# First token group of an attention + feed-forward kernel in units of two f-tiles for 256 tokens, then f-tiles of 512 tokens, six of them in three fp32r passes

## Chip, cores and metric

One core of one Trainium2 chip. The metric is the device time in microseconds of one execution of the program; the median of three executions is given. A profiled execution has a span (first to last instruction) and a time of its own.

## What is computed

The reference runs a recurrent attention (per head a 48 x 48 state that decays by `w`, takes in k v, and is read by r; `u` weighs the token's own k v), and then a feed-forward layer over its output:

```
for t in range(768):                       # 4 sequences, 8 heads of 48
    cur = u*k[t] (x) v[t];  y[t] = r[t] . (state + cur);  state = w*state + k[t] (x) v[t]
x = y as 3072 tokens x 384
h = x @ w_in                               # 384 x 2048
g = h * tanh(log1p(exp(h)))
out = g @ w_out                            # 2048 x 384
```

The two matrices arrive as 64-bit floats, everything else as 32-bit ones.

## The kernel before

**Tokens and groups.** The attention goes in 24 steps `s`; a step makes 128 token columns of x (two chunks of 64). Four steps make a group of T = 512 tokens; there are six groups `g`. The feed-forward layer goes by f-tiles of 128 of the 2048 hidden rows, NF = 16 in a group, so tile number n = 16 g + f. For a tile, `up_tile` (L965) makes h in a PSUM buffer of tag `hp` (two buffers), `evacuate` (L984) copies it to `hb` on ACT or DVE, `gate` (L989) runs sigmoid, arctan and sine on ACT over two tiles (1024 columns; L863, L866, L869, two of them with a table load) and a multiply on DVE (L874 in group 0, L876 later), and `down_tile` (L1019) adds the tile's products to the three accumulators `acc0` to `acc2`. `ffn` (L1078) emits up n, then down n - 6 (LAG), in this order.

**Precision.** In group 0 both products are single fp32 matmuls with whole fp32 weights (L852 up, L896 down); the trace shows each as two records. In groups 1 to 5, x, g and the weights are split into a high and a low fp32r part, and a product is three matmuls (`three`, L828, records at L830).

**Weights.** Each matrix comes in eight pieces of two f-tiles (WG = 2). A piece is loaded as 64-bit numbers (`load_weight`, L334), made fp32 by `convert` (L339: one ACT instruction, L351, and three on DVE, L355, L357, L359), and later split for the fp32r passes by `split` (L364: ACT L372, DVE L374). W_ORDER (L327) is the order of the pieces. A split takes the buffer of the piece before it, so it waits until that was used for the last time.

**The start.** Steps 0 and 1 are loaded first, then pieces of the matrix and steps 2 and 3 (FIRST, L69). Until all four steps are there, group 0 can't take whole 512-token tiles. So `early_pieces` (L929) runs f-tiles 0 to 3 in halves of 256 tokens (records at L945): the half of steps 0 and 1 as soon as these are there, the other half after step 3. EARLY puts two of the four in `hp` and two in the accumulators' banks `acc0` and `acc1`. The attention of steps 0 to 3 is: `dots` (L476), `scores` (L527), `spread_y` (L577, the outputs, in the banks `yt` and `acc2`), `finish` (L741: copies and adds on ACT L760 and DVE L763 make x), and `first_state` (L716, products at L711, copied at L729 and L735). A step's outputs wait for `y` of the step before, which frees the banks. Idle stretches of TensorE that the planner sees are filled with products of zeros (`keep_warm`, L259).

**What sets the order.** The instructions of PE, ACT, DVE, Pool and SP stand in an order that a planner, `Flow` (L91), writes out at build time. Every activity is a thread that asks for an engine with an estimated cost (`dve`, `act`, `pe`, L152 to L161, `tile_cost` L926) and has a rank; of the requests that could start earliest the lowest rank goes first. Each engine then takes its instructions strictly in that order. Steps 4 to 7 are spread over group 0's tiles by `place` (L797) between the shares LO0 and HI0.

Of the kernel before, what the change touches and what calls it, by code (L numbers as in the profile page):

```python
# [67 lines left out]
EARLY = ("hp", "hp", "acc0", "acc1")  # L68
# [21 lines left out]

class Flow:  # L91
# [4 lines left out]
    def __init__(self, free):  # L96
        self.free, self.now, self.events = dict(free), 0.0, {}
        self.live, self.parked, self.fill = [], {}, None

# [35 lines left out]
    def run(self):  # L135
        while self.live:
# [5 lines left out]
            t, th, d = min(todo[e], key=lambda t: (t[0], t[1][0]))  # L142
            self.live = [x for x in self.live if x is not th]
            if e == "pe" and self.fill and t - self.free[e] > WARM_MIN:
                self.fill(t - self.free[e] - LAT)
            self.free[e] = t + d
            self.now = th[1] = t + d + (DMA_LAT if e == "sp" else LAT)
# [4 lines left out]
def dve(cols, fast=False):  # L152
    return {"dve": 0.14 + cols / (1900 if fast else 950)}
# [6 lines left out]
def pe(us):  # L160
    return {"pe": us}  # L161
# [3 lines left out]
def rwkv_mish_kernel(ctx, tc, rkT, rkN, vN, wT, w_in, w_out, consts, rkF, vF, wF, uF, outT):  # L165
# [72 lines left out]
    def token_table():  # L238
# [8 lines left out]
        yield pe(1.0)  # L247
# [10 lines left out]

    def keep_warm(n, out=None):  # L259

        for _ in range(n):
# [12 lines left out]
    idle = ps.tile([128, 512], F32, name="idle", tag="hp", bufs=2)  # L274
    keep_warm(WARM0 - 2)

    flow = Flow(FREE)
# [8 lines left out]
    def check_range():  # L286
# [28 lines left out]
        yield pe(0.3)  # L315
# [11 lines left out]
    W_ORDER = sorted(((i, f) for i in range(2) for f in range(NW)), key=lambda w: w[1] * WG + w[0] * W_SHIFT)  # L327
    raws, whole, parts = {}, {}, {}

# [4 lines left out]
    def load_weight(c):  # L334
        raws[c] = raw = wpool.tile([128, WE, 2], U32, name="wraw", tag="w")
        nc.sync.dma_start(raw, weights(c))
        flow.set(f"issued{c}")
# [26 lines left out]
    def split(c):  # L364
        yield f"whole{c}"
        if c:
            yield f"split{c - 1}"
            yield "used%d,%d" % W_ORDER[c - 1]
        e = whole[W_ORDER[c]]
        yield act(WE)  # L370
        parts[W_ORDER[c]] = w = wpool.tile([128, 2, WE], F32R, name="w", tag="w")
# [3 lines left out]
        flow.set(f"split{c}")  # L375
        flow.set("w%d,%d" % W_ORDER[c])
# [85 lines left out]
    def dots(s):  # L462
        if s < N_SQ:
# [10 lines left out]
            yield pe(1.2)  # L474
# [57 lines left out]
    def attend(s):  # L532
        if s <= B:
# [4 lines left out]
            yield pe(0.6)  # L538
# [101 lines left out]
    def outputs(s):  # L640
# [14 lines left out]
        else:  # L655
            if s >= 2:
                yield f"out{s - 2}"
                yield f"spread{s - 2}"
            engine = yield {**act(96), "dve": 0.25}
# [5 lines left out]
        if not rows:  # L665
            yield pe(0.9 if s < 2 else 1.4)
            ys = spread_y(s)
        else:
            yield pe(2.1 - 0.4 * last)
# [4 lines left out]
        if not rows:  # L674
            flow.start(first_state(s), s - 899.5)
# [40 lines left out]
    def first_state(s):  # L716
        if s >= 2:
            yield f"early{len(EARLY) - 1}"
# [3 lines left out]
        yield pe(0.5)  # L722
# [18 lines left out]
    def finish(s, ys):  # L741
# [9 lines left out]
        if not g:  # L751
            xk = x[:, :, b, 0].rearrange("m k (b t) -> m k b t", b=2)
            parts_y = [y[:, : 2 * KT * CK].rearrange("m (k b t) -> m k b t", k=KT, b=2) for y in ys]
            if s < 2:
                for h in range(2):
                    yield act(192)
                    nc.scalar.copy(out=xk[:, :, h], in_=parts_y[h][:, :, h])
            else:
                yield act(384)
                nc.scalar.copy(out=xk, in_=parts_y[1])  # L760
                for k, h in ((slice(0, 2), slice(0, 2)), (2, 0)):
# [55 lines left out]
    def hp_free(cost=None):  # L817
# [5 lines left out]
        while len(hp_log) >= 2 and hp_log[-2] not in flow.events:  # L823
            yield hp_log[-2]
            yield pe(cost)
# [19 lines left out]
    def up(o, j, event=None):  # L845
        f, T = o.f + j, o.T
        hp = hp_tile("hp", event)
        for k in range(KT):
            fs = slice((k * WG + f % WG) * 128, (k * WG + f % WG + 1) * 128)
            if o.x.dtype == F32:  # L850
                e = whole[0, f // WG]
                nc.tensor.matmul(hp[:, :T], lhsT=e[:, fs], rhs=o.x[:, k, :, 0], start=k == 0, stop=k == KT - 1)  # L852
            else:
                w = parts[0, f // WG]
                three(
                    hp[:, :T], w[:, 0, fs], w[:, 1, fs], o.x[:, k, :, 0], o.x[:, k, :, 1], k == 0, k == KT - 1
                )
# [30 lines left out]
    def down(o, j):  # L888
        f = o.f + j
        for mt in range(KT):  # L890
# [4 lines left out]
            if o.x.dtype == F32:  # L895
                nc.tensor.matmul(a, lhsT=whole[1, f // WG][:, ws], rhs=o.gf[:, j], start=f == 0, stop=f == NF - 1)  # L896
            else:
                w = parts[1, f // WG]
                three(a, w[:, 0, ws], w[:, 1, ws], o.gh[:, j], o.gl[:, j], f == 0, f == NF - 1)
# [26 lines left out]
    def tile_cost(g):  # L926
        return pe(9 * (T + 30) / 2400 if g else 3 * 4 * T / 2400)

    def early_pieces(n):  # L929

        yield f"e0,{n // WG}"
        if n == 3:
            yield "TKn"
        hp = None
        for b in range(0, B, 2):
            yield f"x{b}"
            yield f"x{b + 1}"
            yield pe(1.3)
            flow.fill = None
            if hp is None:  # L940
                hp = hp_tile("hp", f"h{n}") if EARLY[n] == "hp" else ps.tile([128, 512], F32, name="hp", tag=EARLY[n])
            at = slice(b * C, (b + 2) * C)
            for k in range(KT):
                fs = slice((k * WG + n % WG) * 128, (k * WG + n % WG + 1) * 128)
                nc.tensor.matmul(  # L945
                    hp[:, at], lhsT=whole[0, n // WG][:, fs], rhs=xs[0][:, k, b : b + 2, 0], start=k == 0, stop=k == KT - 1
                )
        flow.set(f"early{n}")
        emitted(n, hp)
# [336 lines left out]
```

## Time and profile before

| what | value |
|---|---|
| median of three executions | 501.92 us (501.25 to 502.31) |
| the profiled execution: its time / its span | 499.15 us / 497.4 us |
| TensorE busy | 484.1 us (97%), mean granted clock 0.988 |
| ScalarE busy | 407.5 us (82%) |
| VectorE busy | 356.6 us (72%) |

The time of the profiled execution is 1.75 us above its span; it is 2.77 us below the median. PE stands for matmuls, PEld for weight loads, which lie beside them. L numbers are lines of the kernel before.

### The profile page before, as it was taken

Reading aid. Unit: us, or ns where it says so; the run is one execution under the profiler, and the core shown is the slowest. Engines: PE = TensorE matmul, PEld = TensorE weight load, DVE = VectorE, ACT = ScalarE, POOL = GpSimd, SP = SyncE. Lnnn points to the kernel's source line nnn. Section 1 sums busy time; section 2 is a strip of 40 time slices with the busy share of each in tenths; the row PEclk is TensorE's granted clock in tenths of the full one; section 3 lists DMA queues with packets and bytes.
Section 4 is the critical chain, followed back from the end, with each engine's and each line's share of the span. In section 5 each row is a group of like instructions: output and inputs, shape, how many; then the busy total and the mean of one; then the engine's idle time right before and its main releaser. Section 6 shows DMA issues by size and latency. Waiting matters only on the chain.

```text
span 497.4 us, 11220 instructions
## 1 busy us (share of the span) xinstructions
PE 484.1 (97%) x4779; PEld 369.4 (74%) x4782; DVE 356.6 (72%) x567; ACT 407.5 (82%) x524; POOL 5.4 (1%) x28
## 2 busy tenths in 40 slices
PE   8979999999999999999999999999999999999994
PEld 4766455556678888888888888888888888888872
DVE  6869987978689885687775887685787456465432
ACT  3747988868789898787788899988879988899791
POOL 2000000000000000000000000000000000000000
PEclk9789999999999999999999999999999999999999
DMA  8998122330243021343224445223454103130002
GB/s 314 410 410 359 54 96 91 117 110 5 96 128 111 35 84 29 96 139 108 92 86 144 165 139 184 80 89 150 161 167 138 63 15 129 65 127 1 2 0 70
DMA packets 19978, 60.43 MB, mean 122 GB/s; under 512 B 3088, under 2 KB 3984, under 8 KB 19920
## 3 DMA queue, kind: packets, MB, share of 16 engines
q1 hardware_dynamic: 17184, 54.80, 32.0%
q10 hardware_dynamic: 2736, 4.84, 2.6%
q8 instruction: 39, 0.64, 0.5%
q14 instruction: 19, 0.16, 0.1%
HBM read 52.94 MB, written 4.72 MB: 116 GB/s over the span
## 4 chain that ended last, share of the span: by engine, by line
PE 91%; ACT 3%; DMA 3%; DVE 1%; issue 1%; SPq 0%; ACTq 0%; DVEq 0%
PE hp L830 33%; PE acc L830 30%; PE acc L896 8%; PE hp L852 6%; PE pa L527 2%; PE hp L945 2%; DMA rk<-in_rkT_dram 1%; PE yt L602 1%; PE yh L711 1%; DMA rkn<-in_rkN_dram 1%; PE y L577 1%; PE pa L602 1%; PE pa L614 1%; PE yh L614 1%; PE idle L262 1%; PE pa L476 1%
## 5 line engine op out<-in xcount | busy, mean ns | idle before, releaser
L830 PE MATMUL hp<-x,w 128*128 128x512 f32 x720 | 180.7, 395 | 0.0
L830 PEld LDWEIGHTS hp<-x,w 128*128 128x128 f32 x720 | 133.9, 188 | 30.3 <-issue 2.4
L830 PE MATMUL acc<-gh,w 128*128 128x512 f32 x468 | 156.1, 389 | 0.0
L830 PEld LDWEIGHTS acc<-gh,w 128*128 128x128 f32 x468 | 87.9, 188 | 18.2
L830 PE MATMUL acc<-gl,w 128*128 128x512 f32 x234 | 91.1, 390 | 0.0
L876 DVE TENSOR_TENSOR hb<-hb,fa 128x1024 f32<-128x1024 f32 x40 | 48.9, 1223 | 48.1 <-ACT fa L869 48.0
L863 ACT ACT_TABLE_LOAD x48 | 61.6, 1283 | 4.9 <-DVE gf L874 2.5
L869 ACT ACT_TABLE_LOAD x48 | 61.6, 1283 | 0.8
L986 ACT COPY hb<-hp 128x512 f32<-128x512 f32 x57 | 33.3, 584 | 30.4 <-PE hp L830 23.3
L863 ACT ACTIVATE fa<-hb,small 128x1024 f32<-128x1024 f32 x48 | 55.3, 1152 | 1.8 <-DVE gf L874 1.3
L866 ACT ACTIVATE fa<-fa 128x1024 f32<-128x1024 f32 x48 | 50.9, 1061 | 0.7
L869 ACT ACTIVATE fa<-fa 128x1024 f32<-128x1024 f32 x48 | 50.9, 1060 | 0.5
L830 PEld LDWEIGHTS acc<-gl,w 128*128 128x128 f32 x234 | 43.9, 188 | 9.6 <-DVE gl L884 0.4
L884 DVE TENSOR_TENSOR gl<-hb,gh 128x1024 fp32r<-128x1024 f32 x40 | 48.8, 1220 | 1.6 <-ACT gh L880 1.0
L986 DVE COPY hb<-hp 128x512 f32<-128x512 f32 x39 | 26.9, 690 | 31.5 <-PE hp L830 27.7
L896 PE MATMUL acc<-gf,wraw 128*128 128x512 f32 x96 | 43.8, 592 | 0.0
L896 PEld LDWEIGHTS acc<-gf,wraw 128*128 128x128 f32 x96 | 18.8, 196 | 20.0 <-issue 19.1
L852 PE MATMUL hp<-x,wraw 128*128 128x512 f32 x72 | 33.4, 602 | 0.0
L880 ACT CAST gh<-hb 128x1024 fp32r<-128x1024 f32 x20 | 21.1, 1053 | 11.7 <-DVE hb L876 9.9
L455 DVE TENSOR_TENSOR rk<-rk,TRK 112x1024 f32<-112x1024 f32 x22 | 26.8, 1216 | 0.0
L852 PEld LDWEIGHTS hp<-x,wraw 128*128 128x128 f32 x72 | 13.6, 196 | 14.3 <-issue 13.7
L303 DVE TENSOR_REDUCE small<-we 128x1 f32<-128x768 f32 x16 | 15.1, 947 | 8.1 <-ACT we L301 8.1
(128 smaller groups left out, 560.7 us busy)
## 6 DMA issues: line engine op xcount, KB each, us to landing
wraw<-in_w_in_dram SPq DMA_DIRECT2D x16, 768.0 KB, 6.3
wraw<-in_w_out_dram SPq DMA_DIRECT2D x16, 768.0 KB, 7.9
rk<-in_rkT_dram SPq DMA_DIRECT2D x22, 512.0 KB, 4.3
rkn<-in_rkN_dram SPq DMA_DIRECT2D x20, 384.0 KB, 4.9
v<-in_vN_dram SPq DMA_DIRECT2D x22, 256.0 KB, 4.2
out_dram<-ob ACTq DMA_DIRECT2D x12, 256.0 KB, 2.1
x<-x SPq DMA_DIRECT2D x60, 32.0 KB, 1.9
out_dram<-we ACTq DMA_DIRECT2D x5, 256.0 KB, 5.6
```

The lines of the kernel that those rows point to most:

```text
L303: v.tensor_reduce(out=to[:, 0:1], in_=e, axis=AX.X, op=ALU.min)
L455: nc.vector.tensor_tensor(out=rk[:112].rearrange("d a p (b t) -> d (a p) b t", b=2), in0=rk[:112].rearrange("d a p (b t) -> d (a p) b t", ...
L830: nc.tensor.matmul(out, lhsT=a, rhs=m, start=first and n == 0, stop=last and n == 2)
L852: nc.tensor.matmul(hp[:, :T], lhsT=e[:, fs], rhs=o.x[:, k, :, 0], start=k == 0, stop=k == KT - 1)
L863: nc.scalar.activation(o.g, o.hb, AF.Sigmoid, bias=bias_ln2, scale=1.0)
L866: nc.scalar.activation(o.g, o.g, AF.Arctan)
L869: nc.scalar.activation(o.g, o.g, AF.Sin, scale=2.0)
L876: nc.vector.tensor_tensor(out=o.hb, in0=o.hb, in1=o.g, op=ALU.mult)
L880: (nc.scalar.copy if engine == "act" else nc.vector.tensor_copy)(out=o.gh, in_=o.hb)
L884: nc.vector.tensor_tensor(out=o.gl, in0=o.hb, in1=o.gh.bitcast(F32), op=ALU.subtract)
L896: nc.tensor.matmul(a, lhsT=whole[1, f // WG][:, ws], rhs=o.gf[:, j], start=f == 0, stop=f == NF - 1)
L986: (nc.scalar.copy if engine == "act" else nc.vector.tensor_copy)(out=o.hb[:, j], in_=h)
```

## The change

- Group 0 is no longer 16 tiles of 512 tokens but 16 units (UNITS): four units of two f-tiles (f-tiles 0 to 7) for the 256 tokens of steps 0 and 1, the same four for the 256 tokens of steps 2 and 3, and then f-tiles 8 to 15 for 512 tokens. A unit fills one `hp` bank of 512 columns. Units go down in the same shape. `early_pieces` and EARLY are gone.
- f-tiles 10 to 15 of group 0 go up in three fp32r passes: x of group 0 is split once (`split_x`), and the pieces 5 to 7 of the first matrix are split ahead of all others (S_ORDER).
- The second bank of `spread_y` is an `hp` buffer instead of `acc2`; the zero products write `acc0`.
- W_ORDER sorts by the first unit that uses a piece, so the order of loads changes with it.
- The planner models instruction blocks of TensorE (`fetched`), may let an urgent thread go first within 0.25 us (PATIENCE, URGENT), and has other costs and ranks.
- The scratch for dynamic DMAs is set to 2048 bytes.

```diff
-EARLY = ("hp", "hp", "acc0", "acc1")
+AHEAD = 4
+UNITS = [(h, c) for h in range(2) for c in range(AHEAD)] + [(None, f) for f in range(WG * AHEAD, NF)]
+def split_early(w):
+    return not w[0] and WG * w[1] >= FROM
+def first_use(c):
+    return UNITS.index((0, c) if c < AHEAD else (None, WG * c))
...
+HT = 2 * C
+FROM = 10
+X_SPLIT = 0
+CONVERT = (-999.5, -998.5)
-LO0, HI0, LO1, HI1 = 0.10, 0.80, 0.05, 0.85
+LO0, HI0, LO1, HI1 = 0.10, 0.75, 0.05, 0.85
+BLOCK0, BLOCK, FETCH, LOADING = 449, 256, 6.0, 48.0
+PATIENCE, URGENT = dict(dve=0.25, act=0.25, pe=0.25), -900
+RANK = dict(token_table=-998.6, keys=-998.9, first_state=-899.5)
-COST = dict(dve=1.5)
+COST = dict(dve=1.2)
-L_ATT, L_V, L_IN, L_OUT, L_GATE, L_EVAC, L_PUT, L_FIN = 3, -2, 6, 8, 2, 12, 9, 4
+L_ATT, L_V, L_IN, L_OUT, L_GATE, L_EVAC, L_PUT, L_FIN = 2, -2, 7, 8, 2, 4, 9, 8
...
-    W_ORDER = sorted(..., key=lambda w: w[1] * WG + w[0] * W_SHIFT)
+    W_ORDER = sorted(..., key=lambda w: first_use(w[1]) + w[0] * W_SHIFT)
+    S_ORDER = sorted(W_ORDER, key=lambda w: not split_early(w))
...
-        ys = [ps.tile([128, 512], F32, name=f"y{n}", tag=tag) for n, tag in enumerate(("yt", "acc2"))]
+        ys = ps.tile([128, 512], F32, name="y", tag="yt"), hp_tile("yh", f"half{s}")
...
+    def split_x():
+        for s in range(B):
+            yield f"x{s}"
+        x_parts.append(work.tile([128, 2, KT, T], F32R, name="xp", tag="xp", bufs=1))
+        for k in range(KT):
+            ...
+            yield act(T)
+            nc.scalar.copy(out=xh, in_=xk)
+            yield dve(T)
+            nc.vector.tensor_tensor(out=xl, in0=xk, in1=xh.bitcast(F32), op=ALU.subtract)
+        flow.set("parts")
+    def up_unit(n):
+        h, c = UNITS[n]
+        hp = hp_tile("hp", f"h{n}")
+        if h is None and c >= FROM:
+            w, xp = parts[0, c // WG], x_parts[0]
+            for k in range(KT):
+                fs = ...
+                three(hp, w[:, 0, fs], w[:, 1, fs], xp[:, 0, k], xp[:, 1, k], k == 0, k == KT - 1)
+            return hp
+        for i in range(1 if h is None else WG):
+            f = c if h is None else c * WG + i
+            at, steps = (slice(0, T), slice(0, B)) if h is None else (slice(i * HT, (i + 1) * HT), slice(2 * h, 2 * h + 2))
+            for k in range(KT):
+                fs = ...
+                nc.tensor.matmul(
+                    hp[:, at], lhsT=whole[0, f // WG][:, fs], rhs=xs[0][:, k, steps, 0], start=k == 0, stop=k == KT - 1
+                )
+        return hp
+    def down_unit(n, g):
+        h, c = UNITS[n]
+        for mt in range(KT):
+            ...
+            for i in range(1 if h is None else WG):
+                ...
+                nc.tensor.matmul(
+                    accs[mt][:, at], lhsT=whole[1, f // WG][:, ws], rhs=g[:, of], start=not n and not i, stop=n == NF - 1,
+                    skip_group_check=True,
+                )
...
     def up_tile(n):
         g, f = divmod(n, NF)
         b, j = divmod(n, FB)
-        if n < len(EARLY):
-            yield f"early{n}"
-            return
-        if f == 0:
+        if not g:
+            h, c = UNITS[n]
+            for s in range(B) if h is None else range(2 * h, 2 * h + 2):
+                yield f"x{s}"
+            three_pass = h is None and c >= FROM
+            if three_pass:
+                yield "parts"
+            c = c if h is not None else c // WG
+        elif f == 0:
...
-        yield f"w0,{f // WG}" if g else f"e0,{f // WG}"
+        yield f"w0,{f // WG}" if g else f"w0,{c}" if three_pass else f"e0,{c}"
...
-    nc = _bacc.Bacc("TRN2", target_bir_lowering=False, num_devices=1)
+    nc = _bacc.Bacc("TRN2", target_bir_lowering=False, num_devices=1, dynamic_dma_scratch_size=2048)
```

## Rows read from the trace of the kernel before

**Rows 1.** The profile page: span, and busy time of the engines with their share of it and instructions.
```profile
span 497.4 us, 11220 instructions
PE 484.1 (97%) x4779; PEld 369.4 (74%) x4782; DVE 356.6 (72%) x567; ACT 407.5 (82%) x524; POOL 5.4 (1%) x28
```

**Rows 2.** Busy time by stretch: the stretch, its length, busy us of PE, PEld, DVE, ACT and Pool with their instructions, granted clock, DMA share, GB/s.
```profile
22.00:40.00 18.00, 14.38 (x323) 11.87 (x322) 12.77 (x23) 8.99 (x26) 0.00 (x0) 0.91 1.02 410
40.00:145.00 105.00, 105.00 (x1112) 60.34 (x1111) 91.11 (x147) 88.81 (x116) 0.53 (x6) 1.00 0.30 102
145.00:471.00 326.00, 326.00 (x3003) 269.74 (x3003) 227.31 (x356) 283.38 (x331) 1.38 (x15) 1.00 0.31 103
471.00:497.40 26.40, 19.13 (x82) 14.84 (x80) 8.95 (x10) 14.34 (x15) 0.00 (x0) 0.96 0.09 33
```

**Rows 3.** The chain of work that ended last, in order of time, from 22 to 63 us: start, us, what.
```profile
22.84 1.41 PE hp L945 x6
24.25 0.51 PE pa L711 x32
24.76 1.50 PE hp L945 x6
...
35.60 2.92 PE y L577 x96
...
38.54 0.49 ACT x L760
39.03 0.02 issue
39.05 0.43 DVE x L763
39.48 0.04 issue
39.53 5.46 PE hp L945 x24
...
54.61 2.58 PE acc L896 x6
57.18 2.58 PE hp L852 x6
```

**Rows 4.** Waits of PE from 22 to 40 us: engine, line, what it waited for, us in total, times, longest.
```profile
PE y L577 <- issue: 1.8, 1, 1.8
PE hp L945 <- DVE x L763: 1.0, 1, 1.0
PE pa L711 <- DVE S L729: 0.5, 1, 0.5
PE y L577 <- DVE x L763: 0.3, 1, 0.3
```

**Rows 5.** PE in order of time: start, us, line, operation, in brackets the idle time before it and what ended it.
```profile
28.09 1.57 PE L945 MATMUL hp<-x,wraw 128*128 128x256 f32 x6
...
32.92 0.56 PE L577 MATMUL y<-P,pre 64*64 64x64 f32 x11 [1.77 <-issue]
33.41 1.91 PE L945 MATMUL hp<-x,wraw 128*128 128x256 f32 x6
```

**Rows 6.** DMA from 30.3 to 33.0 us, by queue and kind: packets, MB, share of 16 engines.
```profile
q1 hardware_dynamic: 249, 1.05, 97.8%
q8 instruction: 1, 0.02, 2.6%
```

**Rows 7.** Two stretches, columns as in rows 2.
```profile
30.90:32.80 1.90, 0.25 (x13) 0.17 (x5) 0.59 (x1) 0.00 (x0) 0.00 (x0) 1.00 1.00 389
34.50:37.90 3.40, 3.12 (x85) 2.44 (x85) 3.40 (x6) 1.42 (x3) 0.00 (x0) 0.50 1.02 411
```

**Rows 8.** The chain further on, where group 0's last tiles and group 1's first ones alternate: start, us, what.
```profile
109.83 2.58 PE acc L896 x6
112.40 2.08 PE hp L830 x9
```

**Rows 9.** ACT and DVE by line from 40 to 145 us: count, busy us and mean ns, idle time before and what ended it.
```profile
L351 ACT ACTIVATE wraw<-wraw 128x768 f32<-128x768 uint32 x10 | 9.1, 924 | 0.0
L355 DVE TENSOR_SCALAR we<-wraw 128x768 uint32<-128x768 uint32 x11 | 6.1, 551 | 0.0
L357 DVE SCALAR_TENSOR_TENSOR we<-wraw,we 128x768 uint32<-128x768 uint32 x11 | 10.4, 950 | 0.0
L359 DVE CUSTOM_DVE_ANT_0 wraw<-wraw,we 128x1536 uint16<-128x1536 uint16 x12 | 11.4, 952 | 0.0
L372 ACT CAST w<-wraw 128x768 fp32r<-128x768 f32 x9 | 8.0, 885 | 0.6 <-DVE w L374 0.6
L374 DVE TENSOR_TENSOR w<-wraw,w 128x768 fp32r<-128x768 f32 x9 | 8.5, 949 | 0.0
L986 ACT COPY hb<-hp 128x512 f32<-128x512 f32 x13 | 7.6, 582 | 8.5 <-PE hp L852 4.9 <-PE hp L945 2.1 <-PE hp L830 1.5
L986 DVE COPY hb<-hp 128x512 f32<-128x512 f32 x9 | 6.2, 690 | 5.7 <-PE hp L852 3.7 <-PE hp L830 2.1
```

**Rows 10.** DVE in order of time: the third DVE step of the weight pieces 2 and 3, and one wait.
```profile
30.54 0.95 DVE L359 CUSTOM_DVE_ANT_0 wraw<-wraw,we 128x1536 uint16<-128x1536 uint16 x1
34.03 0.42 DVE L763 TENSOR_TENSOR x<-y,x 128x256 f32<-128x256 f32 x1 [2.54 <-ACT x L760]
...
35.84 0.95 DVE L359 CUSTOM_DVE_ANT_0 wraw<-wraw,we 128x1536 uint16<-128x1536 uint16 x1
```

**Rows 11.** ACT in order of time: the first table load of a gate.
```profile
43.05 1.28 ACT L863 ACT_TABLE_LOAD   x1
```

**Rows 12.** A stretch, columns as in rows 2.
```profile
40.00:60.00 20.00, 20.00 (x151) 11.68 (x150) 19.33 (x32) 17.95 (x20) 0.00 (x0) 1.00 0.52 202
```

More of the change, by code (lines that the diff above doesn't have):

```diff
@@ L142, in run @@
             t, th, d = min(todo[e], key=lambda t: (t[0], t[1][0]))
+            soon = [o for o in todo[e] if o[0] <= t + PATIENCE.get(e, 0.0) and o[1][0] < min(th[0], URGENT)]
+            if soon:
+                t, th, d = min(soon, key=lambda t: (t[1][0], t[0]))
             self.live = [x for x in self.live if x is not th]
@@ L323, in check_range @@
         flow.set("counted")
-    W_ORDER = sorted(((i, f) for i in range(2) for f in range(NW)), key=lambda w: w[1] * WG + w[0] * W_SHIFT)
+    W_ORDER = sorted(((i, f) for i in range(2) for f in range(NW)), key=lambda w: first_use(w[1]) + w[0] * W_SHIFT)
+    S_ORDER = sorted(W_ORDER, key=lambda w: not split_early(w))
     raws, whole, parts = {}, {}, {}
+    for key in S_ORDER:
+        raws[W_ORDER.index(key)] = wpool.tile([128, WE, 2], U32, name="wraw", tag="w")
     def weights(c):
@@ L334, in load_weight @@
     def load_weight(c):
-        raws[c] = raw = wpool.tile([128, WE, 2], U32, name="wraw", tag="w")
-        nc.sync.dma_start(raw, weights(c))
+        nc.sync.dma_start(raws[c], weights(c))
         flow.set(f"issued{c}")
@@ L362, in convert, with split @@
         flow.set("e%d,%d" % W_ORDER[c])
[L364 to L369, printed above, removed]
+    def split(n):
+        key = S_ORDER[n]
+        yield f"whole{W_ORDER.index(key)}"
+        if n:
+            yield f"split{n - 1}"
+            if not split_early(S_ORDER[n - 1]):
+                yield "used%d,%d" % S_ORDER[n - 1]
+        e = whole[key]
         yield act(WE)
-        parts[W_ORDER[c]] = w = wpool.tile([128, 2, WE], F32R, name="w", tag="w")
+        parts[key] = w = wpool.tile([128, 2, WE], F32R, name="w", tag="w")
         nc.scalar.copy(out=w[:, 0], in_=e)
@@ L717, in first_state @@
         if s >= 2:
-            yield f"early{len(EARLY) - 1}"
+            yield f"u{AHEAD}"
         yield f"keys{s}"
@@ L849, in up @@
             fs = slice((k * WG + f % WG) * 128, (k * WG + f % WG + 1) * 128)
[L850 to L857, printed above, removed]
+            w = parts[0, f // WG]
+            three(hp[:, :T], w[:, 0, fs], w[:, 1, fs], o.x[:, k, :, 0], o.x[:, k, :, 1], k == 0, k == KT - 1)
         return hp[:, :T]
@@ L894, in down @@
             a = accs[mt][:, : o.T]
[L895 to L899, printed above, removed]
+            w = parts[1, f // WG]
+            three(a, w[:, 0, ws], w[:, 1, ws], o.gh[:, j], o.gl[:, j], f == 0, f == NF - 1)
     def out_buffer(mt):
@@ L926, in tile_cost @@
     def tile_cost(g):
[L927 to L942, printed above, removed]
-            for k in range(KT):
-                fs = slice((k * WG + n % WG) * 128, (k * WG + n % WG + 1) * 128)
+        return pe(9 * (T + 33) / 2400, 18) if g else pe(3 * 4 * (T + 3) / 2400, 18)
@@ L951, in emitted, with used @@
+    def used(n, i):
+        h, c = UNITS[n]
+        if h == 1:
+            flow.set(f"used{i},{c}")
+        elif h is None and c % WG == WG - 1:
+            flow.set(f"used{i},{c // WG}")
     def emitted(n, h):
@@ L961, in emitted @@
             flow.set(f"ups{g}")
-        if not g and f % WG == WG - 1:
-            flow.set(f"used0,{f // WG}")
+        if not g:
+            used(n, 0)
     def up_tile(n):
@@ L1025, in down_tile @@
                     yield f"put{g - 1},{mt}"
-            else:
-                for k in range(2, len(EARLY)):
-                    yield f"h{k}"
-        yield f"w1,{f // WG}" if g else f"e1,{f // WG}"
+        if g:
+            yield f"w1,{f // WG}"
+        else:
+            yield "e1,%d" % (UNITS[n][1] // (WG if UNITS[n][0] is None else 1))
         yield f"g{n}"
         yield tile_cost(g)
-        down(batches[b], j)
+        if g:
+            down(batches[b], j)
+        else:
+            down_unit(n, batches[b].gf[:, j])
         if j == FB - 1:
             flow.set(f"downs{b}")
-        if not g and f % WG == WG - 1:
-            flow.set(f"used1,{f // WG}")
+        if not g:
+            used(n, 1)
         if f == NF - 1:
```

98 lines of the change are left out of this document (67 added, 31 removed).

## The prediction

> **What bounds the kernel now.** I read the page first: TensorE is busy 97% of the span, ScalarE 82%, VectorE 72% [rows 1]. An average hides the stages, so the busy time by stretch comes next [rows 2]. From 40 to 471 us PE is busy in every microsecond (105.00 of 105.00, 326.00 of 326.00): there only less PE work shortens the run. The last 26.4 us hold 7.3 us of PE idleness, in the last gates, which the change does not touch. What is left is the start: from 22 to 40 us PE is busy 14.38 of 18.00 us. The chain of waits says why [rows 3]: the half tiles of steps 0 and 1 are used up, and the second halves start only at 39.53 us, behind step 3's products (35.60), its ScalarE copy (38.54) and its VectorE add (39.05). So **x of step 3, ready near 39.5 us, is the event that ends the start**; behind it PE never waits. The question is how much feed-forward work stands before it, and how much PE work there is in all.
>
> **A. Work brought ahead of step 3.** Before, four half tiles stand there (the first at 22.84 us, the last at 33.41 [rows 3, 5]). After, four units that need only steps 0 and 1 can stand there; a unit is two half tiles. The second halves of before give the price: 24 records in 5.46 us, so 1.37 us a half tile and 2.73 us a unit [rows 3]. Four units are 10.92 us against 5.46, so 5.46 us of work move ahead of step 3. They gain only as far as they fill time that PE loses there now; the rest delays step 3.
>
> What PE loses from 22 to 40 us: 18.00 - 14.38 = 3.62 us idle [rows 2], which the waits split into 1.8 us in step 2's products with no releaser, 0.5 us for a state copy, and 1.0 + 0.3 us for the adds that make x [rows 4]. [...] Together 5.3 us. [...] The 1.3 us for x I leave in, since by then the units may be used up. So step 3 comes 5.46 - 4.0 = 1.46 us later and 5.46 us less work is behind it: **-4.0 us**. Ends: 0 (everything inserted delays step 3) and -5.3.
>
> **The stall by itself.** At 32.92 us PE resumes inside one matmul group after 1.77 us with no releaser [rows 5]. Around it the data queues hold 97.8% of the DMA engines, and one packet of PE's or another engine's instructions is among the traffic [rows 6]. I read this as PE out of instructions while their block stands in the DMA traffic. A unit issues 24 instructions (12 weight loads, 12 products) in 2.73 us, step 3's products 192 in 2.92 us [rows 3]; units spread between the attention's bursts give a block time to land. They also add 4 x 12 = 48 instructions ahead of step 3, so block boundaries shift, and a second stall of 1.8 us is the other end.
> [...]
>
> **B. Three passes.** A group-0 up tile takes 2.58 us in fp32 [rows 3], a three-pass one 2.08 us [rows 8]. Six of them: 6 x 0.50 = **-3.0 us**, all on PE behind 39.5 us.
>
> **C. Halves cost more.** Two half tiles take 2.73 us where a whole one takes 2.58 [rows 3], +0.15 us. Up: eight f-tiles in halves instead of four, +0.6. Down: eight instead of none, 8 x 0.15 = +1.2. Together **+1.8 us**.
>
> **D. Splits.** x of group 0 costs three ScalarE copies and three VectorE subtractions of 512 columns: by the evacuations of that size 0.58 and 0.69 us [rows 9], so 1.7 us on ACT and 2.1 on DVE. The splits of pieces 5 to 7 (0.89 and 0.95 us each [rows 9]) are moved earlier, not added, and the loads are the same sixteen in another order. Cover: from 40 to 145 us ACT is idle 16.2 of 105 us and DVE 13.9 [rows 2]. That stage gets about 5 us shorter, which takes as much of either's idleness; but the first gate, which now begins at 43.05 us [rows 11], can begin once two units are up, and ACT is idle 9.0 us and DVE 5.2 from 22 to 40 [rows 2]. I put it at **0**; without cover it is the 2.1 us of DVE.
>
> **E. The rest.** `spread_y` and the units now share two `hp` banks, so a step's outputs wait for the evacuation of the tile before the last (0.58 us on ACT). PE has other units to run only if their order allows it; 0, up to 4 x 0.58 = 2.3 us for the steps 0 to 3. The new ranks and costs move work of ACT and DVE only where PE does not wait today (40 to 471 us): 0; the loss, if there is one, is that of rivals 3 and 4. The planner's clock and the scratch size issue no instruction: 0.
>
> **Sum.** -4.0 - 3.0 + 1.8 = -5.2 us. The profiled execution would go from 499.15 to 493.95 us; it stood 2.77 us under its median, and I take the same below the new one: 501.92 - 5.2 = **496.7 us**. With A at its ends the sum is -1.2 to -6.5 us, so 495.4 to 500.7 us; a second stall of 1.8 us on top of A = 0 would make it 502.5, which I count with rival 3. Below that, down to 493.4, I allow 2 us for the first 22 us, whose order changes too and which I did not cost.
>
> **Rivals.**
> 1. *The units can't be fed early.* They need pieces 2 and 3 of the first matrix, which before came out of DVE only at 31.5 and 36.8 us [rows 10]; until 39.5 us PE used pieces 0 and 1 alone. If they stay there, two units (5.46 us, as before) run in the window and A falls to what the tile order gives by itself: B + C = -1.2 us and perhaps 0.5: 500.2 us. For it: DVE is in strict order and waits 2.54 us for ScalarE in this window [rows 10]. Against it: that same wait, and 5.2 us of DVE idleness, are room for the 2.45 us (0.55 + 0.95 + 0.95 [rows 9]) that a piece needs. The same time results if the planned order puts the units behind step 3, so that the change does not do what it says.
> 2. *The stall stays.* Then A is 4.0 - 1.8 = 2.2 us, the sum -3.4, the time 498.5 us. [...]
> 3. *No change (500.9 to 502.9 us).* ACT and DVE, at 85% and 87% from 40 to 145 us and at 90% and 97% from 40 to 60 [rows 2, 12], can't be pressed into less, and PE gets waits of the size of what it saves.
> 4. *Slower: the three-pass units wait for their weights.* PE takes its instructions in order; a three-pass unit needs the piece in fp32, its split, and x split. One piece's chain is 0.92 + 2.45 + 0.89 + 0.95 = 5.2 us [rows 9] on two engines with little room. While PE stands before such a unit, the downs and the attention of steps 4 to 7 stand behind it. For pieces 5, 6 and 7 late by half the chain it is 3 x 2.6 = 7.8 us, and 496.7 + 7.8 = 504.5 us. It decides from 5.2 us in all, 1.7 us a piece. For it: DVE's 97%. Against it: the three pieces are loaded by then (DMA share 0.30 from 40 us on [rows 2]), and the units stand some 25 us behind 40 us.
>
> **Chances.** The forecast 0.58, rival 1 0.12, rival 2 0.10, rival 3 0.08, rival 4 0.12. A measurement of this kernel can tell about 0.2% (1.0 us) from no change. Forecast and rivals 1 and 2 are faster by more: 0.80. Same 0.08, slower 0.12. The range goes from 493.4 us to 501.9: it holds the forecast, rivals 1 and 2 and half of rival 3, and leaves out the slower case and the other half.
>
> **What would show it.** Right: from 22 to 40 us PE is busy nearly all the time at full clock, with four units (48 records of 256 columns) before step 3's x; the first gate begins well before 43 us; the unit that follows step 3 starts between 39 and 42 us; nine records of 512 columns for each of f-tiles 10 to 15 with 2.1 us; no PE wait behind that. Wrong: a wait of PE with no releaser of over 1 us in this window (rival 2), units that wait for DVE L359 (rival 1), waits of the three-pass units for L374 or `xp` (rival 4), waits on `g` or evacuations between 40 and 140 us (rival 3). A change of the tail, or of groups 1 to 5, would contradict the argument as a whole.

## The result: slower, by 0.9%

| | before | after |
|---|---|---|
| median | 499.75 us (498.44 to 504.24, 20 runs) | 504.63 us (503.25 to 506.22, 20 runs) |
| ratio, 95% interval | | 1.0089 [1.0071, 1.0107] |
| profiled execution: time / span | 499.15 / 497.4 us | 504.99 / 503.2 us |
| mean granted clock | 0.988 | 0.979 |

The forecast was 496.7 us with 501.9 as upper end, 5.2 us under the 501.92 of three executions; over 20 executions the kernel before stands at 499.75, and the change adds 4.9 us. The forecast was wrong in sign. 504.6 us is the number of rival 4, but not its mechanism. A trace shows one execution, and executions of one kernel differ with the granted clock (the kernel before took 498.2 us at 0.990 and 503.3 us at 0.979).

### The profile after

The page, to set beside [rows 1]:
```profile
span 503.2 us, 11402 instructions
PE 484.3 (96%) x4873; PEld 388.8 (77%) x4876; DVE 379.6 (75%) x611; ACT 380.7 (76%) x465; POOL 5.3 (1%) x28
```
TensorE is busy 0.2 us longer than before; the span grew by 5.8 us. So nearly all of the growth is idleness, and the busy time by stretch (columns as in [rows 2]) says where:
```profile
22.00:40.00 18.00, 14.17 (x258) 11.54 (x257) 12.99 (x23) 10.57 (x27) 0.00 (x0) 0.81 1.01 403
40.00:60.00 20.00, 14.88 (x226) 12.74 (x228) 12.49 (x24) 12.07 (x22) 0.00 (x0) 0.74 0.43 177
60.00:120.00 60.00, 60.00 (x740) 47.95 (x729) 59.25 (x99) 51.17 (x65) 0.36 (x4) 1.00 0.31 98
...
471.00:503.20 32.20, 24.57 (x106) 19.35 (x104) 9.86 (x10) 18.78 (x20) 0.00 (x0) 0.94 0.08 27
```
From 22 to 60 us PE is idle 3.83 + 5.12 = 8.95 us; before it was 3.62, all ahead of 40 us [rows 2, 12]. The rest is as it was: 2.36 us up to 22 (2.44 before), 7.63 in the tail (7.27), none between. Sum +5.6 us. VectorE, 59.25 us of 60 from 60 to 120 (52.19 before), has no room left, but PE doesn't wait there.

The chain of waits over the same stretch as [rows 3]:
```profile
31.46 3.11 issue
34.57 0.21 PE yh L627
...
35.49 1.28 ACT L911
36.78 1.15 ACT fa L911
37.95 0.27 ACT first L787
...
40.87 0.37 ACT x L813
41.26 0.56 DVE x L817 x2
41.81 0.13 DVE first L712
41.96 0.38 PE y L627 x2
...
45.20 3.16 issue
48.35 0.47 PE yh L627 x2
48.83 7.10 PE hp L1006 x24
```
Three things stand here. Twice PE stops inside step 2's and step 3's products (L627; L577 before) for over 3 us with no releaser ("issue"), where [rows 5] had one stop of 1.77. Between them ScalarE runs the first gate (L911 and, left out here, L914) and conversions ahead of step 2's copy of x (L813); behind that copy come VectorE's adds (L817) and the spread copy (L712), which puts columns of v into `first` for step 3's products. And the unit that follows step 3's products starts at 48.83 us. It is the fourth unit of steps 0 and 1: only three (36 records) stand ahead of these products, not four. x of step 3 is ready at 49.9 us, against 39.5 before. PE's waits from 22 to 60 us say the same ([rows 4] before):
```profile
PE yh L627 <- issue: 6.3, 2, 3.2
PE y L627 <- DVE first L712: 2.2, 1, 2.2
```
**Where the stops stand.** Counting TensorE's records, loads and matmuls together, in order of start: before, the stop comes behind record 958; after, the two come behind 958 and 1214. The distance is 256, and the changed kernel's own planner works with blocks of 256 (BLOCK) that end at 705, 961 and 1217. In each stop one packet of the instruction queue q8 is among the DMA traffic (the stop of 31.47 to 34.57, columns as in [rows 6]; here q14 has one too):
```profile
q1 hardware_dynamic: 259, 1.09, 95.3%
q8 instruction: 1, 0.02, 2.2%
q14 instruction: 1, 0.01, 0.7%
```
The q8 packets start at 32.14 and 45.81 us, and PE goes on 2.4 and 2.5 us later; before, 30.40 and 32.92, 2.5 us. The planner assumes 6.0 us from the crossing of one block to the next block's arrival (FETCH). Here record 705 was reached at 29.43 and 961 at 34.58 us, 5.2 us later, but 1217 only at 48.36, 13.8 us behind 961. The delay lies ahead of the packet: it starts 11.2 us behind record 961, when PE has already stood for 0.6 us; the one before started 2.7 us behind record 705.

**The clock.** Behind or around the stops it is at 0.50 (columns as in [rows 2]):
```profile
35.30:38.50 3.20, 3.20 (x11) 2.54 (x9) 0.80 (x1) 2.95 (x4) 0.00 (x0) 0.50 1.03 422
42.10:52.20 10.10, 6.94 (x104) 6.01 (x104) 5.72 (x9) 3.40 (x5) 0.00 (x0) 0.50 0.65 264
```
A third such stretch, 3.4 us long, begins at 25.0 us, although PE had waited at most 0.53 us at a time in the ten us ahead of it. In all that level lasts 17.1 us up to 60 us, against 10.2 before. It explains why the two units from 48.83 on take 7.10 us for 24 records instead of 5.46 [rows 3]: 3.45 of the 7.10 us lie at 0.50, and half of that is 1.7. From 22 us on 13.5 us of PE's busy time lie in such stretches, against 3.1 before [rows 7]; half of the difference, 5.2 us, is more than the 3.0 us that the three passes take off the busy time.

**ScalarE in order of time**, the place to which the prediction gave no cost:
```profile
35.49 1.28 ACT L911 ACT_TABLE_LOAD   x1 [5.55 <-PE yh L627]
36.78 1.15 ACT L911 ACTIVATE fa<-hb,small 128x1024 f32<-128x1024 f32 x1
37.95 0.27 ACT L787 COPY first<-S 48x96 f32<-48x96 f32 x1
...
40.77 0.45 ACT L813 COPY x<-yh 128x384 f32<-128x384 f32 x1
```
The first gate writes `fa`, a buffer that shares its place with `pre`, which step 2's products still read. The planner knows nothing of that and put the gate ahead of the copies L787 and L813. So ScalarE stands 5.55 us until those products (delayed by the first stop) are done, and then the copy of step 2's x stands another 5.3 us behind the gate.

**The units themselves** (chain, 85 to 95 us; PE in order of time, 62 to 71 us), against [rows 3, 8]:
```profile
85.34 2.27 PE hp L884 x9
87.61 2.59 PE acc L1020 x12
90.20 2.08 PE hp L884 x9
92.28 2.59 PE acc L1020 x12
```
```profile
62.85 2.75 PE L1020 MATMUL acc<-gf,wraw 128*128 128x256 f32 x12
65.44 2.75 PE L1006 MATMUL hp<-x,wraw 128*128 128x256 f32 x12
68.03 2.75 PE L1020 MATMUL acc<-gf,wraw 128*128 128x256 f32 x12
```
A three-pass tile takes 2.08 us as predicted. Two half tiles in a full stream take 2.59 us (distance of starts), a whole tile 2.58: halves cost next to nothing.

### The profile page after: what moved, and what is told of

It reads as the page before. It is cut to its first block, busy times and chain, and to the rows that moved or that the text cites. A ratio compares the mean times of both kernels' runs of the same rounds, so it can differ in the third digit from the quotient of the medians.

```text
span 503.2 us, 11402 instructions
## 1 busy us (share of the span) xinstructions
PE 484.3 (96%) x4873; PEld 388.8 (77%) x4876; DVE 379.6 (75%) x611; ACT 380.7 (76%) x465; POOL 5.3 (1%) x28
## 4 chain that ended last, share of the span: by engine, by line
PE 88%; ACT 4%; DMA 4%; issue 2%; SPq 1%; DVE 1%; ACTq 0%; DVEq 0%
PE hp L884 35%; PE acc L884 29%; PE acc L1020 8%; PE hp L1006 5%; DMA wraw<-in_w_out_dram 2%; PE pa L577 2%; DMA kn<-in_rkN_dram 2%; PE yt L652 1%; PE yh L763 1%; PE pa L664 1%; PE pa L652 1%; ACT L911 1%; PE yh L664 1%; PE yh L627 1%; ACT fa L911 1%
## 5 line engine op out<-in xcount | busy, mean ns | idle before, releaser
L924 DVE TENSOR_TENSOR hb<-hb,fa 128x1024 f32<-128x1024 f32 x40 | 48.8, 1221 | 39.6 <-ACT fa L917 39.5
L1072 DVE COPY hb<-hp 128x512 f32<-128x512 f32 x57 | 39.3, 690 | 32.0 <-PE hp L884 29.4
L911 ACT ACTIVATE fa<-hb,small 128x1024 f32<-128x1024 f32 x48 | 55.3, 1153 | 6.9 <-DVE hb L924 6.4
L914 ACT ACTIVATE fa<-fa 128x1024 f32<-128x1024 f32 x48 | 50.8, 1059 | 0.9
L884 PEld LDWEIGHTS acc<-gl,w 128*128 128x128 f32 x234 | 43.9, 188 | 9.5 <-DVE gl L932 0.4
L1020 PE MATMUL acc<-gf,wraw 128*128 128x256 f32 (+1 forms) x144 | 43.9, 450 | 0.0
L1072 ACT COPY hb<-hp 128x512 f32<-128x512 f32 x39 | 22.8, 585 | 20.1 <-PE hp L884 16.1
L1020 PEld LDWEIGHTS acc<-gf,wraw 128*128 128x128 f32 x144 | 28.2, 196 | 10.9 <-issue 8.4
L1006 PE MATMUL hp<-x,wraw 128*128 128x256 f32 (+1 forms) x108 | 33.1, 465 | 0.0
L1006 PEld LDWEIGHTS hp<-x,wraw 128*128 128x128 f32 x108 | 24.0, 228 | 5.7 <-issue 1.9
L928 DVE CAST gh<-hb 128x1024 fp32r<-128x1024 f32 x32 | 22.1, 691 | 2.0 <-PE acc L884 0.2
L398 ACT ACTIVATE wraw<-wraw 128x768 f32<-128x768 uint32 x16 | 14.7, 923 | 8.8 <-DMA wraw<-in_w_in_dram 8.8
```

The costliest lines, as they stand in the source:

```text
L398: nc.scalar.activation(r, low, AF.Copy, bias=2.0, scale=2.0**-51)
L884: nc.tensor.matmul(out, lhsT=a, rhs=m, start=first and n == 0, stop=last and n == 2)
L911: nc.scalar.activation(o.g, o.hb, AF.Sigmoid, bias=bias_ln2, scale=1.0)
L914: nc.scalar.activation(o.g, o.g, AF.Arctan)
L924: nc.vector.tensor_tensor(out=o.hb, in0=o.hb, in1=o.g, op=ALU.mult)
L928: (nc.scalar.copy if engine == "act" else nc.vector.tensor_copy)(out=o.gh, in_=o.hb)
```

## Experiments

Three theories (their letters are not those of the prediction's terms). **Blocks (F)**: the stops are TensorE out of instructions at the ends of 256-record blocks, and where these ends fall decides. **Order (O)**: the gate ahead of x of step 2 (and what it delays) is the loss. **VectorE (D)**: the change leaves VectorE without room, and what is gained early is given back by late copies. Ratios are against the kernel before, with 95% intervals. "Records shifted" means 84 zero products of 128 columns at the start in place of 21 of 512, the same columns and 126 records more; the planner isn't told, and the order of all other instructions stays.

### First four: gate, loads, blocks, passes

`gate_told`: the first gate also waits for `pre`'s last reader.
```diff
+            yield "out2"      # in the first gate, ahead of its request for ACT
```


> Edit: the first gate's thread also waits for the planner's event that step 2's products are issued; PE's order up to step 3's products stays the same, on ScalarE the copy of step 2's x and the spread copies come ahead of the first gate. Theory O (the order on ScalarE is the main cause: the gate needs the buffer that step 2 still reads, and step 2's copy stands behind it, 40.77 instead of about 35.5 us): step 3's x comes 4 to 5 us earlier than 48.8 us, the time falls from 504.6 to about 499 or 500 us. Theory F (PE runs out of instructions at block boundaries): step 3's products start earlier but then stand as long before their instructions come; the start of the unit behind step 3 stays near 48 us, the time within 1.5 us of 504.6.


Measured: 507.24 us, 1.0164 [1.0116, 1.0212]. The order is mended: x of step 2 stands ahead of the gate.
```profile
34.91 0.48 ACT L813 COPY x<-yh 128x384 f32<-128x384 f32 x1 [1.60 <-PE yh L627]
35.41 1.28 ACT L911 ACT_TABLE_LOAD   x1
```
The wait for the spread copy is gone, the first stop stays (3.1 us), the second falls to 0.8 us, and the unit after step 3 starts 5.6 us earlier (43.20). Up to 60 us PE idles 6.1 us, against 11.3 in the changed kernel. Yet the time rises, because PE then waits between 111 and 117 us for the transfer that completes x of step 7:
```profile
PE hp L884 <- DMA x<-x: 5.7, 1, 5.7
```
Neither O nor F had foreseen this wait, from which D was formed. In its stage the order is worth 5.2 us, and the late x takes them back; from the time alone O can't be judged.

`told_late`: gate_told, and the weight pieces 5 to 15 are loaded only behind step 3's last product; the loads of step 4, which stand in the same list, come later too.
```diff
-    ("rk", 3), ("v", 3), ..., ("rkn", 2), ("rkn", 3), ("raw", 5), ("raw", 6), ("raw", 7),
+    ("rk", 3), ("v", 3), ..., ("rkn", 2), ("rkn", 3),
...
+    ("rk", 4), ("rkn", 4), ("v", 4), ("raw", 5), ("raw", 6), ("raw", 7), ..., ("raw", 15),
...
-        yield "out2"              # in load_rest
+        yield "out3"
...
+        if c == 5:
+            tc.add_manual_dep(ins.ins, last_y[3].ins.name, sync, reason="loads behind step 3")
```


> Edit: as gate_told, and the weight pieces 5 to 15 are loaded only behind the last product of step 3, so that the DMA queues are nearly empty from about 30 us until then. Theory F with the DMA traffic as its cause: both PE stalls of 3.1 us inside the products of steps 2 and 3 vanish or shrink to under 1.5 us, the unit behind step 3 starts at 38 to 41 us, and the time is 495 to 498 us, if no later piece comes too late. Theory O alone: the stalls were not what mattered, the time is that of gate_told or, with the pieces late, 2 to 5 us above it. If the stalls are not fetches held up by the DMA traffic, they stay at 3.1 us.


Measured: 506.93 us, 1.014 [1.0101, 1.018], where F with the DMA traffic as cause had 495 to 498. From 22 to 40 us the DMA share is 0.26, and the two stops are still there at the same records as in gate_told: the first takes 1.3 us (3.1 there), the second 1.5 (0.8 there). Record 961 now comes 3.4 us after 705. The second line is the second stop, at a DMA share of 0.00:
```profile
22.00:40.00 18.00, 14.71 (x364) 13.04 (x363) 15.03 (x26) 12.83 (x31) 0.00 (x0) 1.00 0.26 85
39.77:41.26 1.49, 0.00 (x0) 0.00 (x0) 0.00 (x0) 0.00 (x0) 0.00 (x0) 1.00 0.00 0
```
PE's longest wait of this kind from 22 to 50 us:
```profile
PE yh L628 <- issue: 2.8, 2, 1.5
```
So data traffic does not make the stops; that it lengthens them only the first one suggests. The time says nothing here: from 60 to 120 us PE is busy 53.84 of 60 us, most of the rest being x of step 7 as in gate_told, and 0.9 us a late split of weights.
```profile
PE hp L885 <- DMA x<-x: 4.3, 1, 4.3
```

`aligned`: the changed kernel with records shifted, nothing else.
```diff
-    keep_warm(WARM0 - 2)
+    for _ in range(4 * (WARM0 - 2)):
+        nc.tensor.matmul(
+            idle[:, :128], lhsT=zeros.broadcast_to([128, 128]), rhs=zeros.broadcast_to([128, 128]), start=True, stop=True
+        )
```


> Edit to the changed kernel: 84 products of zeros of 128 columns in place of 21 of 512 at the very start, 126 more TensorE instructions in the same time, everything else and every order unchanged. Theory F: instruction number 961 of the old count is now reached in the unit before step 2 and the boundary behind it in the middle of step 2's products; the stalls move to other instructions and change in length, together by more than 1.5 us in either direction, and the time by 1.5 to 4 us. Theory O, or stalls that belong to the matmuls and not to their place in the instruction stream: the stalls stay at the same matmuls and the time within 1 us of 504.6.


Measured: 498.94 us, 0.9985 [0.9962, 1.0008], that is 5.7 us less than the changed kernel (5.2 by the ratios; 1.5 to 4 were expected, with stops that move). What is left of PE's waits from 22 to 160 us, but for 0.3 us:
```profile
PE y L630 <- DVE first L715: 3.3, 1, 3.3
PE hp L1009 <- issue: 0.4, 1, 0.4
```
6.3 us of stops became none at a block's end (the 0.4 us stand at record 1132), by nothing but records that stand elsewhere: that block ends make the stops is shown. Up to 60 us PE idles 5.9 us. The wait that O speaks of, for the spread copy, is still there (3.3 us).

`no_three`: FROM = 16, no three passes in group 0.
```diff
-FROM = 10
+FROM = 16
```


> Edit to the changed kernel: no f-tile of group 0 in three passes (the constant 16 in place of 10), so no split of x and no early split of weights. By term B of the prediction (six tiles at 2.58 instead of 2.08 us): 3.0 us slower than the changed kernel, 507.6 us. If the early splits cost as much on the other engines as the passes save: no slower, 503 to 505 us.


Measured: 510.6 us, 1.0219 [1.0179, 1.0258], 6.0 us slower than the changed kernel where 3.0 were expected. The stops are there as in the changed kernel (5.5 us in all, 6.3 there). PE's busy time grows by 4.6 us, more than the 3.0 of the passes, and from 60 to 160 us it loses 0.56 + 1.62 = 2.2 us, to x's transfers (1.6) among others: the new order is part of it, so the 3.0 can't be read from the time alone.

### Both mended, and before with shifted records

`told_aligned`: gate_told with records shifted.
```diff
+    for _ in range(4 * (WARM0 - 2)):   # as in aligned
...
+            yield "out2"                   # as in gate_told
```


> Edit: the two edits of gate_told and aligned together. Theory F and O together (stalls at block boundaries in step 2's and 3's products, and behind them step 2's copy queued behind the first gate): both waits are gone, the unit behind step 3 starts near 37 to 39 us instead of 48.8. If what is gained there stayed, the time would be 494 to 495 us. But in the run of gate_told VectorE was busy over 95% from 60 us on and the x of step 7 came 5.7 us too late for group 1. Theory D (VectorE bounds group 0 once the start is short): that wait of PE for the x copies grows to 6 to 9 us, and the time is 499 to 502 us, no better than aligned alone.


Measured: 504.93 us, 1.0077 [1.004, 1.0114]; even the 499 to 502 of theory D were missed. The early part is better than in any run up to here (unit after step 3 at 40.50 us; PE idle 5.5 us up to 60), and `PE hp L887 <- DMA x<-x` takes 5.7 us at the same place as in gate_told. What is won early is lost to x of step 7; VectorE is busy 59.38 of 60 us there.

`before_shift`: the kernel before with 121 zero products of 89 columns, 200 records more, nothing else.
```diff
-    keep_warm(WARM0 - 2)
+    for _ in range(121):
+        nc.tensor.matmul(idle[:, :89], ..., rhs=zeros.broadcast_to([128, 89]), start=True, stop=True)
```


> Edit to the kernel before: 121 products of zeros of 89 columns in place of 21 of 512 at the very start, 200 more TensorE instructions in the same time, all orders unchanged. The boundary that lay in step 2's products (1.8 us stall) then lies just ahead of them, the next one at the start of step 3's. Theory F: the stall of 1.8 us is gone or moved to step 3's start and shorter, with it the low clock behind it; 1.5 to 3.5 us faster than the kernel before (0.993 to 0.997). If the stall belongs to step 2's products and not to their place in the instruction stream: it stays at 1.8 us and the time is the same within 0.2%.


Measured: 497.35 us, 0.9943 [0.9904, 0.9982]. The stop of [rows 5] is gone, the lower clock of [rows 7] too, and the second halves start at 36.67 us instead of 39.53. A stop of 0.85 us now stands one block earlier, at record 703 (20.50 us). PE's longest waits from 22 to 60 us, and behind them a row of the chain:
```profile
PE hp L948 <- DVE x L766: 1.5, 1, 1.5
PE y L580 <- DVE x L766: 0.6, 1, 0.6
```
```profile
36.67 5.46 PE hp L948 x24
```
The kernel before owed its own stall to the same thing, and moving records by itself takes it away, but for the one of 0.85 us.

`told_aligned_c`: told_aligned with the planner's factor on VectorE's cost at 1.5 (as in the kernel before) instead of 1.2.
```diff
-COST = dict(dve=1.2)
+COST = dict(dve=1.5)
```


> Edit: told_aligned with the planner's weight of VectorE's time at 1.5 instead of 1.2, so 38 evacuations instead of 57 stand on VectorE and 82 instead of 62 on ScalarE (rows of the program; rows hold up to two). Theory D: the wait of PE for step 7's x shrinks by 2 to 4 us against told_aligned, the time to 496 to 498 us. If the late x is a matter of order and not of VectorE's load: no change against told_aligned.


Measured: 496.75 us, 0.9934 [0.9906, 0.9963], the fastest of the twelve kernels with the change. x of step 7 comes in time: PE is busy in every microsecond from 40 to 160, VectorE 55.40 of 60 from 60 to 120. Of stops 0.40 us are left, at record 958. The chain ahead of step 3 now runs along VectorE:
```profile
33.71 0.96 DVE we L407
...
35.05 0.95 DVE wraw L409
36.00 0.46 DVE x L820 x2
36.47 0.13 DVE first L715
36.61 0.24 PE y L630
...
39.01 3.85 PE hp L1009 x12
```

### One part of told_aligned_c at a time, and two more

`gate_told_c`: without the shifted records.
```diff
-    for _ in range(4 * (WARM0 - 2)):
...
+    keep_warm(WARM0 - 2)
```


> Edit: told_aligned_c without the small products at the start, so with the changed kernel's places of the instruction blocks. Theory F: the stall of about 3 us in step 2's products and one of about 1 us in step 3's are back, the unit behind step 3 starts 4 us later than 39.0, and since VectorE no longer holds up group 1 the time follows: 499.5 to 501.5 us, 3 to 5 above told_aligned_c. If the blocks did not matter any more: 496 to 497.5 us.


Measured: 499.6 us, 0.9994 [0.9964, 1.0024]. Stops of 1.9 and 3.2 us behind records 958 and 1214 are back (about 3 and 1 were expected), the unit after step 3 starts at 44.11 us; +2.9 us, as F has it.

`aligned_c`: without the gate's wait.
```diff
-            yield "out2"
```


> Edit: told_aligned_c without the first gate's wait, so with ScalarE's order of the changed kernel. Theory O as a term of its own: step 3's products wait 3.3 us instead of 2.3 us as in aligned, the unit behind them starts about 1 to 3 us later than 39.0: 497.5 to 500 us. If the order on ScalarE costs nothing once the stall ahead of it is gone: 496 to 497.5 us.


Measured: 501.93 us, 1.0063 [1.0039, 1.0087]; +5.2 us by the medians (6.4 by the ratios), where at most 500 us were expected. The wait for the spread copy is 3.1 us (2.3 with the gate's wait), and x of step 7 is late again, by 2.5; the clock stands at 0.50 from 37.8 to 44.6 us (to 41.1 with it). So with shifted records the wait that O speaks of is worth 0.8 us, and more is in what follows: clock and plan.

`ahead2_c`: AHEAD = 2, two units ahead of step 3 instead of four.
```diff
-AHEAD = 4
+AHEAD = 2
```


> Edit: told_aligned_c with two pairs of half units instead of four (the constant 2 in place of 4), so as much work ahead of step 3 as before the change. By the prediction's terms A and C: 5.46 us of work move behind step 3, of which the window had room for about 4.0, and four f-tiles less go in halves up and down (-1.2 us): 2.8 us slower than told_aligned_c, 499 to 500.5 us. If the early units only push step 3 back (A at zero): 1.2 us faster, 495 to 496 us.


Measured: 502.25 us, 1.0084 [1.0055, 1.0113]; +5.5 us by the medians (7.5 by the ratios) where 2.8 were expected. PE is busy 12.04 us from 22 to 40 instead of 14.88; its wait for the spread copy is 5.1 us:
```profile
PE y L630 <- DVE first L715: 5.1, 1, 5.1
PE hp L887 <- DMA x<-x: 0.9, 1, 0.9
```
The clock of 0.50 lasts 10.2 us (33.6 to 43.9) instead of 3.4. In this frame early units do fill time that is otherwise lost, as term A said; but this too is a new plan, and the 0.9 us for x belong to it.

`inf_sp`: told_aligned_c, with the planner's count started 126 records later (so that it knows the shifted blocks) and the spread copies of v on ScalarE alone.
```diff
-    flow = Flow(FREE, 2 * WARM0)
+    flow = Flow(FREE, 2 * WARM0 + 126)
...
-            engine = yield {**act(96), "dve": 0.25}
+            engine = yield act(96)
```


> Edit: told_aligned_c, and the planner's count of TensorE instructions starts at 172 instead of 46, the number that is really issued, so that it no longer puts work ahead of step 2's x for a stall that isn't there; and the copies of v's last columns stand on ScalarE alone. Theory: in told_aligned_c VectorE is busy 17.5 of 18 us from 22 to 40 us and step 3's products wait 2.3 us for such a copy behind it; this wait shrinks to under 1 us, the low clock behind it goes, 1 to 3 us faster than told_aligned_c: 494 to 496 us. If VectorE's conversions bound that window by their amount: the same within 0.2%.


Measured: 504.54 us, 1.0102 [1.0058, 1.0145]: missed. The early part was as hoped up to 40 us (PE 17.29 of 18 us busy from 22 to 40), but new waits came: 2.4 us for step 3's add, 1.6 without releaser (at record 3007, eight blocks behind 958), and 2.8 for x in three places (PE 54.93 of 60 us from 60 to 120).

`after_c`: the changed kernel with the factor 1.5 alone.
```diff
-COST = dict(dve=1.2)
+COST = dict(dve=1.5)
```


> The changed kernel with the planner's factor on VectorE's cost at 1.5 instead of 1.2, and nothing else: neither the small products at the start nor the first gate's wait. TensorE's order is the same up to the units behind step 3, ScalarE's up to the first gate, so blocks and gate stand as in the changed kernel; only what follows step 3 is planned anew. Theory (the loss lies ahead of step 3, in blocks and gate): waits without releaser of 6 us in all in the products of steps 2 and 3, the first gate again ahead of step 2's x copy (first table load behind a wait of about 5 us), the unit after step 3 at 47 to 49 us, and a time of 503 to 507 us, as the changed kernel (504.6): by the kernel with factor 1.5, gate and shifted blocks (496.8) plus 2.9 for the blocks plus 5.2 for the gate it is 504.9. Rival (the loss is the planned order behind 40 us, with VectorE saturated from 60 to 120 us): the early part as before, but VectorE at 55 to 57 of 60 us from 60 to 120, and 497 to 501 us.


Measured: 510.07 us, 1.0222 [1.0184, 1.0259]: early losses as in the changed kernel, as expected (6.2 us of stops, 2.3 for the spread copy, the unit after step 3 at 47.95), and on top 2.5 us for x of step 7 and 1.9 us more of busy PE time, which the expectation of 503 to 507 did not have.

**The eight together.** Three switches, all combinations: the ratio, and behind it PE's idle time up to 60 us in the trace:

| | records as they were | records shifted |
|---|---|---|
| changed kernel | 1.0089; 11.3 us | 0.9985; 5.9 us |
| gate waits | 1.0164; 6.1 us | 1.0077; 5.5 us |
| factor 1.5 | 1.0222; 10.5 us | 1.0063; 7.3 us |
| both | 0.9994; 8.2 us | 0.9934; 5.9 us |

Shifting records gains in every row, 0.6 to 1.6% (3.0 to 7.9 us). The other two have no price of their own: the gate's wait costs 0.7 to 0.9% with factor 1.2 and gains 1.3 to 2.3% with 1.5. Both change the planned order of everything behind, and whether x of step 7 is late then weighs as much as the early part. Up to 60 us, with factor 1.2, either edit takes off over 5 us and both together hardly more: blocks and gate lengthen the same waits (the second stop shrinks from 3.2 to 0.8 us when the gate waits), so the early loss can't be shared out between them.

## Why the prediction was wrong, step by step

**What bounds the kernel.** The place was right: the start up to step 3's x. "Behind it PE never waits" held in the changed kernel (none from 60 to 471 us), but eight of the other kernels on its base waited 0.9 to 5.7 us for x between 60 and 160.

**A and the stall: the step that failed.** Of the 5.3 us that it took as lost, the prediction counted 4.0 as time that units fill: 1.8 of stall, 0.5 of a state copy and 1.7 of clock (half of the 3.40 us at 0.50 [rows 7]). It read the stall rightly as missing instructions, but then argued that units between the bursts give a block time to land, and did not count records to see where the blocks end. That a busier PE wins back the 1.7 us of clock no run shows: from 22 to 40 us the clock of `told_late` was 1.00 with PE busy for 14.71 us, that of `inf_sp` 0.91 with 17.29. The blocks end late in step 2's products and at the end of step 3's, bursts of 192 records with nothing put in between; the one stall became two, of 3.1 and 3.2 us. "A second stall of 1.8 us" was named as an end, but at little over half the size and counted as unlikely. The lower clock came with it, 6.8 us more of it. The sign that the prediction named for rival 2, a wait without releaser of over 1 us, came twice. `before_shift` shows the other side: most of those 3.5 us were no room for units, they go away without any unit. Besides, the planned order put one of the four units behind step 3's products, so 2.73 us of work moved ahead of them and not 5.46. That early units fill lost time is seen in `ahead2_c` (2.8 us more idleness of PE from 22 to 40 us, with two units ahead of these products instead of three), but not against the kernel before, which with shifted records idles 2.70 us there and has no more work ahead than `ahead2_c`.

**E.** The shared banks cost nothing that the trace shows. What was missed is another sharing, `fa` with `pre`: the prediction counted the gate's earlier start (D) as relief for ScalarE, and never asked which buffer it writes. Its size depends on the stops. With shifted records PE's wait for the spread copy is 3.3 us in `aligned` and 2.3 in `told_aligned`, so 1.0 us is the gate's and the rest VectorE's chain; with records as they were the gate's wait takes 5.2 us from PE's idle time up to 60 us.

**B** was right (2.58 to 2.08 us). **C** was mis-sized: +1.8 us was taken from 24 records in 5.46 us, a stretch that begins behind an idle PE; in a full stream a pair of halves takes 2.59 us, so C is about +0.1.

**D** held at 0 for PE, by luck of the order: cover fell from 7.8 to 0.75 us of VectorE from 60 to 120 us. Kernels with 59.4 us waited 5.7 us; but `aligned` with 59.02 did not and `inf_sp` with 56.89 did, so the amount alone doesn't decide.

**Rivals.** 1 (units fed late) and 4 (three-pass units wait for weights): no such wait, though of 1 the other half, units planned behind step 3, came true for one unit in four. 2 (the stall stays) was nearest, and too small. 3: VectorE can't be pressed, seen in the runs that moved the rest.

**What the change is worth.** `before_shift` and `told_aligned_c` have only short stops left (0.85 and 0.40 us): 0.9943 [0.9904, 0.9982] and 0.9934 [0.9906, 0.9963], spans of 495.2 and 493.4 us. The second also has the gate's wait and the factor 1.5, and is the best of twelve. With both sides nearly freed of the stops the change gains too little to be told apart here, where B and C by themselves are near 3 us. PE's idle time up to 60 us is 5.3 us in the first and 5.9 in the second: against a kernel before without the stop of [rows 5], A gains nothing that shows. PE's busy time is 482.0 and 479.8 us, so 2.2 of the 3 us arrive there; what takes the rest isn't settled.

**Open.** Why the instruction packet ahead of the second stop starts 11.2 us behind record 961, when the one ahead of the first starts 2.7 us behind 705; whether VectorE's load or the place of step 7 in the order makes x late (no run separates them). A `pre` with a buffer of its own wasn't tried, and the new ranks, PATIENCE and the scratch size were not taken back one by one.

## What to carry over

Before costing any change that adds, removes or moves instructions ahead of a stall without a releaser, count that engine's records up to the stall, and where the same multiple falls in the new order; try a shift by cheap instructions on both kernels, or the two are not compared on equal terms. Ask of each step that starts earlier which buffer it writes and who still reads it. Count in the new order whether the work stands where the estimate puts it. Where a planner orders everything, a small edit is a new order for all that follows, so read each experiment by its stages and not by its total.

## What the hardware showed unexpectedly

In the 14 traces TensorE stopped 18 times for 0.40 us or more, without a releaser, at the end of a block: within 4 records of 958 plus or minus a multiple of 256. The stops took 0.40 to 3.46 us; in the one before the change and the two after it PE went on 2.5, 2.4 and 2.5 us after the start of an instruction packet of q8. The DMA share was 0.98 and 0.93 in the two stops of the changed kernel and 0.00 in the second one of `told_late`. After the first stop the clock fell to 0.50 for 3.4 us before (from 34.5 us) and after the change (from 35.2); in `before_shift`, where only 0.85 us of stop were left (at 20.5 us), it was 1.00 from 22 to 460 us. The clock also fell to 0.50 at 25.0 us in the changed kernel, with no wait of PE over 0.53 us in the ten us ahead.
